# Backward windowed attention with one job per step, and half of the weight gradients computed between its steps

## The chip, the cores and the metric

The kernel runs on one core of a Trainium2 chip. The metric is the device time in microseconds (us) of one execution. All executions of a kernel lie within 1% of its median. Engines are named as in the profile: PE is the matmul engine (TensorE; "PEld" is its weight load), DVE is VectorE, ACT is ScalarE, POOL is GpSimd and SP is SyncE. "ACTq" or "SPq" in front of a DMA is the time in which that engine's instruction stream stands at the *issue* of the DMA; the engine runs no other instruction of its stream meanwhile.

## The reference

Four layers, A B A B, on x of 2048 x 640, each `x = x + layer(layernorm(x))`. A is linear attention, B is softmax attention in a window of 256 positions, both with 32 heads of 20. The kernel returns the output and the gradients of x and of the four weights.

```python
def _B_ref(x, wqkv, wo):                       # A_ref, layernorm: cut
    q, k, v = ...                              # (x @ wqkv), 32 heads of Dh = 20
    scores = einsum("bhqd,bhkd->bhqk", q, k) * Dh ** -0.5
    mask = (i - j >= 0) & (i - j < 256)
    p = softmax(where(mask, scores, -1e9))
    o = einsum("bhqk,bhkd->bhqd", p, v)
    return o... @ wo

def reference(A_x, A_wqkv, A_wo, B_wqkv, B_wo, B_x, grad_out):
    _out, _vjp = jax.vjp(_f, A_x, A_wqkv, A_wo, B_wqkv, B_wo)
    return (_out, *_vjp(grad_out))             # cut
```

## The kernel before

The forward pass comes first (about 900 us). The backward pass then goes through layers 3 (B), 2 (A), 1 (B), 0 (A). For each B layer there is a stage of its own, the attention backward. It walks over 128 units: a unit is four heads (group g of 8) and one block of 128 queries (b of 16), with the at most three key blocks that its window touches. Per unit it recomputes scores and their exponentials `e` (ScalarE), multiplies dP with e into `ds` (VectorE), transposes half of ds by DMA and the other half on PE, and multiplies ds, its transpose and e into dq, dk and dv.

```python
for s in range(n + LAG):                                  # LAG = 5; one step per unit
    if s < n and units[s][1] == 6 and ...: load(units[s][0] + 1)   # slabs of the next group, on ScalarE's queue
    sa = scores(s, 0, "QT", "KT");      pb = scores(s - 2, 1, "dOT", "VT")
    expo(s, 0, sa);                     dscore(s - 2, 1, pb)
    sb = scores(s, 1, "QT", "KT");      pa = scores(s - 1, 0, "dOT", "VT")
    expo(s, 1, sb);                     dscore(s - 1, 0, pa)
    dvk(s - 2, ...)                                       # dk, dv: own accumulator and copy
    if (s - LAG) % 2 == 1: dq([s - LAG - 1, s - LAG])     # dq: own accumulator, in pairs

def dscore(u, half, ps):
    nc.vector.tensor_tensor(out=dv[:, hs], in0=ps..., in1=ev[:, hs], op=ALU.mult)   # ds
    if half == 0:
        self.tr(dsT_of[u]..., ds_of[u]...)                # transposed by DMA
    else:
        for i in range(nb):
            nc.tensor.transpose(tp..., ds_of[u]..., self.ident)   # on PE, right behind its ds
        ...                                               # copied by VectorE or ScalarE in turn
```

dO is loaded once per stage (2.5 MB), and the results of all groups stay on chip in one tile `dqkv`. The next stage (`dh`) transposes that tile and stores it to DRAM for the weight gradients. Those run at the very end, the two layers of a kind in one accumulation:

```python
def weight_grads(self, ls, out_dW, out_dWo):              # called with (3, 1), then (2, 0)
    for m in range(DT):
        ps = pps.tile([P, 512], F32, name="wg")[:, 0:w]
        for i in range(len(ls)):
            for tt in range(TT):
                nc.tensor.matmul(ps, lhsT=lhs[i][:, tt, m * P:(m + 1) * P], rhs=rhs[i][:, tt, :], ...)
        ...                                               # copy to bf16, store
```

The softmax here doesn't subtract the row's maximum and nothing guards it: scores larger than these inputs give would overflow.

## Time and profile before

| | before |
|---|---|
| median of the first 3 runs | 3235.71 us (3222.08 to 3236.21) |
| profiled span | 3230.4 us |
| attention backward, layers 3 and 1 (first score to last product) | 474.1 us each, 3.70 us per unit |
| from the last product to the first matmul of the next stage | 50.1 and 47.3 us |
| weight gradients (first matmul to end) | 421.4 us |

The share of busy time of an engine says little here, since stages have different limits; so here are the windows of the three stages that the change touches. This view gives for each stretch its length, the busy time of PE, PEld, DVE, ACT and POOL with the number of their instructions, then the TensorE clock that was granted (1.00 is full speed), the mean share of time in which DMA engines were busy, and GB/s.

```profile
core 0: us, PE busy (x) PEld busy (x) DVE busy (x) ACT busy (x) POOL busy (x), PEclk, DMA share, GB/s
998.80:1472.90 474.10, 376.98 (x6064) 239.22 (x6063) 258.70 (x320) 280.33 (x496) 147.49 (x240) 0.50 0.58 112
1939.60:2413.70 474.10, 376.62 (x6064) 239.06 (x6064) 258.68 (x320) 280.31 (x495) 147.48 (x240) 0.50 0.58 112
2809.00:3230.40 421.40, 355.53 (x1920) 190.41 (x1920) 21.69 (x36) 12.35 (x24) 0.00 (x0) 0.91 0.45 147
```

No engine is full in the attention stages, and PE runs at half clock throughout, although it is "busy" for 80% of the time. In the weight gradients PE is the limit: 355 us of 421, at nearly full clock.

What PE waits for in layer 3 is in the groups: this view of one line's instructions shows the six transposes of a unit, and what ended PE's idle time before them.

```profile
L745 PEld LDWEIGHTS <-ds x720: 102/147/152, 1004.0 to 1468.1; 128*128 128x128 bf16 x180
L745 PE MATMUL acc<-ident,ds x720: 286/314/314, 1004.0 to 1468.2; 128*128 128x128 bf16 x180
its engine sat idle before it (us, times) until:
  DVE ds L735: 150.6, 195
```

PE and its weight load together sit 150.6 us in front of the transposes, waiting for the ds that VectorE is just writing (the two overlap in part, so it is not a sum of lost time).

The chain that ended last shows the end: matmuls in a row, and between them loads that nothing hides.

```profile
2792.26 16.46 DMA wg_r_38523<-dqkv_118
2808.95 132.40 PE wg L895 x640
...
2950.46 10.38 DMA wg_r_39271<-g_114
...
2961.40 45.14 PE wg L895 x320
```

And between attention and the next stage PE stands idle for 50 us. SP's timeline shows the transposing load of the weight, WT:

```profile
1472.87 40.33 SPq L132 DMA_TRANSPOSE WT_23077<-in_B_wqkv_dram  x1
```

```profile
1472.88 4.91 ACTq L126 DMA_DIRECT2D dqkv_118<-dqkv  x5
```

### The profile page before, as it was taken

To read this page: it belongs to the slowest core of one execution; us is meant where nothing else is said; L and a number is where in the kernel's file an instruction comes from. 1 tells how busy PE (TensorE), PEld (TensorE's weight loads), DVE (VectorE), ACT (ScalarE), POOL (GpSimd) and SP (SyncE) were. 2 spreads that over 40 slices of the span, in tenths; PEclk is the share of its full clock that TensorE was granted. 3 is DMA by queue.
4 is the path that set the end of the run, shared out by engine and by line. 5 is a ranking of instruction groups with operands and counts; after the bars stand their busy time and mean duration, and the time that the engine had idled before them with its cause. 6 is when DMAs were issued, how large, how long until landed. Compare 5 with 4: busy or idle time off the path is not lost. (4 is left out here: it accounts for less than half of the span.)

```text
span 3230.4 us, 64877 instructions
## 1 busy us (share of the span) xinstructions
PE 2348.7 (73%) x26304; PEld 1421.8 (44%) x26304; DVE 1400.7 (43%) x2994; ACT 1160.2 (36%) x2233; POOL 765.5 (24%) x1282
## 2 busy tenths in 40 slices
PE   7599984899744777783846747777774747697797
PEld 5355542454422555552533424554542524344344
DVE  6345543443154555551744645555543735300000
ACT  4167762477603555561101105556550101100000
POOL 0144441255512333331221103333331111000000
PEclk9789986888675555555977875555557968898898
DMA  6788954888597555649879987556469889834624
GB/s 201 204 173 180 195 149 137 177 187 175 138 218 187 116 105 99 120 84 163 185 164 171 239 205 148 96 110 109 93 134 168 172 165 199 259 116 145 205 88 144
DMA packets 992204, 510.50 MB, mean 158 GB/s; under 512 B 818592, under 2 KB 959904, under 8 KB 990624
## 3 DMA queue, kind: packets, MB, share of 16 engines
q1 hardware_dynamic: 738176, 182.81, 36.8%
q10 hardware_dynamic: 242976, 286.83, 29.1%
q0 software_dynamic: 10752, 36.71, 4.7%
q8 instruction: 206, 3.38, 0.4%
q14 instruction: 94, 0.77, 0.1%
HBM read 175.51 MB, written 147.98 MB: 100 GB/s over the span
## 5 line engine op out<-in xcount | busy, mean ns | idle before, releaser
L735 DVE TENSOR_TENSOR ds<-sp,e 128x768 bf16<-128x768 f32 (+2 forms) x512 | 456.4, 906 | 419.5 <-PE sp L702 274.5
L716 ACT ACTIVATE e<-sp 128x768 bf16<-128x768 f32 (+2 forms) x512 | 377.2, 770 | 241.1 <-DMA dOT<-dOT_133 117.4
L343 ACT ACTIVATE e<-s 128x768 bf16<-128x768 f32 (+2 forms) x512 | 374.0, 774 | 140.2 <-PE s L341 109.4
L720 POOL TENSOR_SCALAR_AFFINE_SELECT e<-e 128x512 bf16<-128x512 bf16 x256 | 163.1, 637 | 707.8 <-issue 534.8
L702 PE MATMUL sp<-KT,QT 32*128 32x384 bf16 (+2 forms) x1024 | 247.8, 484 | 95.8 <-DMA VT<-qkvT_132 37.8
L567 PEld LDWEIGHTS <-dqkvT 128*128 128x128 bf16 x1920 | 200.1, 106 | 259.9 <-issue 97.6
L702 PE MATMUL sp<-VT,dOT 32*128 32x384 bf16 (+2 forms) x1024 | 262.0, 471 | 58.2 <-ACT e L716 45.6
L745 PE MATMUL acc<-ident,ds 128*128 128x128 bf16 x1440 | 199.8, 308 | 100.4 <-DVE ds L735 99.6
L346 POOL TENSOR_SCALAR_AFFINE_SELECT e<-e 128x512 bf16<-128x512 bf16 x256 | 163.4, 638 | 398.8 <-ACT e L343 395.4
L569 ACT ACTIVATE dh_junk<-d 128x320 bf16<-128x320 f32 x128 | 56.0, 437 | 505.1 <-PE d L567 492.7
L745 PEld LDWEIGHTS <-ds 128*128 128x128 bf16 x1440 | 132.2, 136 | 210.2 <-DVE ds L735 201.4
L899 DVE CAST wg_r<-wg 128x480 bf16<-128x480 f32 (+1 forms) x36 | 21.7, 603 | 415.1 <-PE wg L895 355.8
L341 PE MATMUL s<-ring 32*128 32x128 bf16 x2880 | 166.0, 234 | 18.5 <-ACT e L343 17.3
L901 ACT CAST wg_r<-wg 128x480 bf16<-128x480 f32 (+1 forms) x24 | 12.4, 515 | 423.3 <-PE wg L895 345.0
L515 PEld LDWEIGHTS <-gT 128*128 128x128 bf16 x640 | 67.6, 112 | 186.0 <-DMA gT<-car 142.7
L349 POOL TENSOR_SCALAR_AFFINE_SELECT e<-e 128x512 bf16<-128x512 bf16 x224 | 143.8, 642 | 0.0
L724 POOL TENSOR_SCALAR_AFFINE_SELECT e<-e 128x512 bf16<-128x512 bf16 x224 | 142.7, 637 | 0.0
L341 PEld LDWEIGHTS <-ring 32*128 32x128 bf16 x2880 | 82.9, 97 | 127.1 <-issue 119.1
L779 ACT CAST dqkv<-acc 128x160 bf16<-128x160 f32 x224 | 70.2, 313 | 190.3 <-PE acc L757 190.3
L215 PEld LDWEIGHTS <-ln_hnT 128*128 128x128 bf16 x960 | 96.1, 106 | 95.1 <-DMA ln_hnT<-ln_hn 37.9
L202 DVE TENSOR_TENSOR car<-d,car 128x320 bf16<-128x320 f32 x128 | 62.2, 486 | 159.2 <-PE d L200 158.8
L702 PEld LDWEIGHTS <-dOT 32*128 32x128 bf16 x1024 | 66.1, 100 | 147.6 <-issue 143.5
(588 smaller groups left out, 4540.6 us busy)
## 6 DMA issues: line engine op xcount, KB each, us to landing
qkvT_128<-ring ACTq DMA_DIRECT2D x16, 768.0 KB, 6.3
qkvT_132<-ring ACTq DMA_DIRECT2D x16, 768.0 KB, 4.4
dqkv_118<-dqkv ACTq DMA_DIRECT2D x16, 480.0 KB, 3.9
dqkv_117<-dqkv_t ACTq DMA_DIRECT2D x16, 480.0 KB, 5.2
dqkv_116<-dqkv ACTq DMA_DIRECT2D x16, 480.0 KB, 4.5
dqkv_115<-dqkv_t ACTq DMA_DIRECT2D x16, 480.0 KB, 4.9
out_dram<-car ACTq DMA_DIRECT2D x32, 160.0 KB, 4.5
out_dram<-wg_r ACTq DMA_DIRECT2D x40, 120.0 KB, 1.7
```

The source lines that it names most:

```text
L215: nc.tensor.matmul(ps, lhsT=hnT[:, k, :], rhs=W[:, k, ci * HD:(ci + 1) * HD], start=(k == 0), stop=(k == self.DT - 1))
L341: nc.tensor.matmul(ps[:, j, i * P:(i + 1) * P], lhsT=ring[r0:r0 + HP, G + g, kt * P:(kt + 1) * P], rhs=ring[r0:r0 + HP, g, qs], start=True ...
L343: nc.scalar.activation(ev[:, 2 * half:2 * half + 2], ps[:, :, 0:nkt * P].rearrange("p h (i q) -> p h i q", q=P), ACT.Exp, scale=self.c_att)
L346: nc.gpsimd.affine_select(out=ev[:, :, nkt - 1, :], in_=ev[:, :, nkt - 1, :], compare_op=ALU.is_ge, fill=0.0, base=0, pattern=[[0, 4], [1, ...
L349: nc.gpsimd.affine_select(out=ev[:, :, 0, :], in_=ev[:, :, 0, :], compare_op=ALU.is_ge, fill=0.0, base=-1, pattern=[[0, 4], [-1, P]], chan ...
L567: nc.tensor.matmul(ps, lhsT=dT[:, k, :], rhs=WT[:, k, cs], start=(k == 0), stop=(k == self.QTT - 1))
L702: nc.tensor.matmul(ps[:, j, 0:nkt * P], lhsT=slabs[g][ta][r0:r0 + HP, b * P:(b + 1) * P], rhs=slabs[g][tb][r0:r0 + HP, k0 * P:(k0 + nkt) * P],
L716: nc.scalar.activation(ev[:, 2 * half:2 * half + 2], ps[:, :, 0:nkt * P].rearrange("p h (i k) -> p h i k", k=P), ACT.Exp, scale=c_att)
L720: nc.gpsimd.affine_select(out=ev[:, :, nkt - 1, :], in_=ev[:, :, nkt - 1, :], compare_op=ALU.is_ge, fill=0.0, base=0, pattern=[[0, 4], [-1 ...
L724: nc.gpsimd.affine_select(out=ev[:, :, 0, :], in_=ev[:, :, 0, :], compare_op=ALU.is_ge, fill=0.0, base=-1, pattern=[[0, 4], [1, P]], chann ...
L735: nc.vector.tensor_tensor(out=dv[:, hs], in0=ps[:, :, 0:nkt * P].rearrange("p h (i k) -> p h i k", k=P), in1=ev[:, hs], op=ALU.mult)
L745: nc.tensor.transpose(tp[:, i * P:(i + 1) * P], ds_of[u][:, (nb + i) * P:(nb + i + 1) * P], self.ident)
```

## The change

The intent: shorten the attention step by taking away its wait for ds, and use the poorly filled PE of layer 1's attention stage for half of the weight gradients (those of layers 3 and 2, whose inputs are complete by then). Scores of one half of the heads are paired with dP of the other half, as they were. The diff, cut to its core:

```diff
+    def permute_w(self):                       # at the start, on SP's queue: B's weight with
+        w = 4 * DH                             # q, k, v of a group side by side (160-byte runs)
+        for t in range(3):
+            self.dma(out[:, t], in_[:, t], self.nc.sync)
@@ dh
-        self.tr(dT, dqkv)
-        self.dma(self.dqkv_d[l][:, tt, :], dqkv)
+        if dqkv is None:
+            self.tr(dT, self.dqkv_d[l][:, tt, :])      # B layers: transposed from DRAM
@@ seg_attention_bwd
-            dO = p1.tile([P, TT, D], BF, name="dO_ld")
-            self.dma(dO, sv["dO"])
@@ load(g): six slabs and now dO's, all on ScalarE's queue
+                r["dO"] = psl.tile([P, TT, 4 * DH], BF, name="dOsl")
+                self.dma(r["dO"], sv["dO"][:, :, 4 * g * DH:4 * (g + 1) * DH])
@@ the step
                 sa = ...; pb = ...; expo(a, 0, sa); dscore(b2, 1, pb)
+                job(s - JL)              # dk, dv and dq of one block, five steps back, one accumulator
+                filling(rate)            # layer 1: 4 weight-gradient matmuls
                 sb = ...; pa = ...; expo(a, 1, sb); dscore(c, 0, pa)
-                dvk(s - 2, ...); dq([...])
+                flip(b2)                 # the PE transposes, out of dscore
+                filling(rate)
@@ job: results leave per group, also on ScalarE's queue
+                if kt == TT - 1:
+                    self.dma(self.dqkv_d[l][:, :, g * 12 * DH:(g + 1) * 12 * DH], outs.pop(g))
@@ run
-                self.seg_attention_bwd(l, dqkv)
+            if l == 3:
+                self.seg_attention_bwd(l, None, 0, 3)          # no fill, 3 score buffers
+            else:
+                    self.seg_attention_bwd(l, it, 4, 2)        # it: wgrad of layers 3, 2
+                    self.drain(it)
-        self.weight_grads((3, 1), ...); self.weight_grads((2, 0), ...)
+            for k in (1, 0):
+                self.drain(self.wgrad(k, pools, True))
@@ wgrad: the first half leaves as fp32 partials in DRAM; the second adds them
+                    if last:
+                        pt = pw.tile([P, 480], F32, name="wg_pt")        # two buffers
+                        self.dma(pt[:, 0:w], part[rows, ...], nc.sync)
+                        nc.vector.tensor_add(o[:, 0:w], ps, pt[:, 0:w])
+                        self.dma(dst, o..., nc.sync)
```

## The prediction

It was made before the changed kernel was built.

> **What bounds the kernel now.** No single engine: the page shows PE 73%, DVE 43%, ACT 36%, DMA unevenly. By stage (windows):
> - The two attention-backward stages run 998 to 1472 and 1940 to 2414 us, 474 us each, 3.70 us per step of 128. PE is busy 79%, ACT 59%, DVE 55%, and the granted clock is exactly 0.50 in every window. The waits there are PE and its weight load waiting for DVE's ds (0.4 and 0.8 us per step: the transposes stand right behind the ds they need) and sp waiting for exp.
> - Weight gradients, 2791 to 3230 us (439 us): 1920 matmuls, clock 0.90. In the chain of waits PE has 355 us (132.4 us per 640 matmuls of 480 columns, 207 ns each); about 80 us are four exposed loads.
>
> **What the change does.**
> 1. Transposes move behind the second score pair, the products become one job five steps back. PE work per step at half clock, estimated from the timeline: two score quads 0.64 us, six transposes 0.64, 36 products of 33 ns 1.2, so about 2.5; ACT about 2.2 and DVE 2.0. With the ds wait gone and three sp buffers I expect 3.05 us per step: about -58 us in layer 3. The 2.5 MB dO load (9.6 to 10.7 us) before the first score goes: -9 us per stage.
> 2. Layer 1's stage gets 8 weight-gradient matmuls per step (about 905 of 960 fit in; the rest hides behind the WT load, 38 to 40 us of SP time). At full clock they cost 1.43 us per step, at half clock 2.9. The skill's page "TensorE: Matmul & The Clock Gate", Part 1, says the throttled state is the default and sustained activity releases it; this trace agrees (0.50 in attention, 1.00 in dense stretches of B-to-A). The fill should release it: scores and transposes halve (0.65 us), products 1.2, fill 1.43, plus about 0.4 for the one wg bank, whose eviction is issued only at the next burst: 3.7 to 3.8 us per step. I expect +10 us less the 9 us of dO.
> 3. The end keeps half the matmuls (177 us of PE), but SP issues both the fp32 partial's load and the output store in order, so a partial's load goes out only after the previous output is ready: about 0.35 + 0.35 + 3 + 0.65 us, 4.3 us per tile against 3.3 of PE; 6 to 6.5 for layer B with its 160-byte output runs. Estimate: 130 + 86 + 2 x 40 + 25 first load and tail = about 290 to 320 us against 439: -150 with some luck in overlap.
> 4. At the start Wp is permuted: 15,360 runs of 160 bytes on SP's queue, ahead of the first LN transposes. "DMA: Bandwidth & Descriptors", Queues, rings and completion order, says descriptors on an engine are consumed in ring order; no view here tests it. 960 per engine at 35 to 60 ns (page: 62 ns per packet on q10): first matmul at 50 us, not 19.8: +30 us.
> 5. dh transposes dqkv from DRAM instead of SBUF; one store moves: about 0. WT's wait stays.
>
> Sum: -58 - 9 + 10 - 9 - 150 + 30 = -186, so about 3045 us.
>
> **Signs.** Layer-3 attention about 410 us, with no ds wait before transposes; layer-1 attention 450 to 540 us with clock above 0.8; end 250 to 320 us with partial loads among its waits; first matmul near 50 us.
>
> **What would make it wrong.** If the fill doesn't release the clock, layer 1 takes 5.5 us per step, +230 us, and the whole is a tie or a loss. ACT could also block on full DMA queues (loads held it 5 to 11 us before). If permutation is cheap and the end PE-bound, 2950.

## The result, and the profile after

The changed kernel has a median of 3073.75 us (3056.17 to 3084.75, 4 runs) against 3235.96 us; the ratio is 0.9489, with a 95% interval of 0.9436 to 0.9542. Ratios in this document are the mean time of one kernel's runs over that of the other's of the same rounds, so they are not quite the ratio of the medians quoted. The prediction's total (about 3045 us) held within 1%. Its terms did not hold as well. The table splits both profiled spans at the same events; "measured" is the difference of the two profiles.

| stretch | before | after | measured | predicted |
|---|---|---|---|---|
| start to first matmul | 19.8 | 35.2 | +15.4 | +30 |
| from there to layer 3's first score | 979.0 | 974.6 | -4.4 | -9 (dO load) |
| layer 3 attention | 474.1 | 457.5 | -16.6 | -58 |
| last product to first dh matmul | 50.1 | 32.0 | -18.1 | 0 |
| layers 3 to 2 to layer 1's first score | 416.7 | 416.1 | -0.6 | -9 (dO load) |
| layer 1 attention, with fill after | 474.1 | 550.2 | +76.1 | +10 |
| last product to first dh matmul | 47.3 | 36.1 | -11.2 | 0 |
| layers 1 to 0 | 347.9 | 354.5 | +6.6 | 0 |
| weight gradients at the end | 421.4 | 198.3 | -223.1 | -150 |
| sum | 3230.4 | 3054.5 | -175.9 | -186 |

(The profiled run of after, 3056 us, is its fastest. The attention stage of layer 1 is the least steady part: runs below that leave its code as it is show 561.0, 569.3 and 571.6 us.)

The windows of the same three stages after the change:

```profile
core 0: us, PE busy (x) PEld busy (x) DVE busy (x) ACT busy (x) POOL busy (x), PEclk, DMA share, GB/s
1009.80:1467.30 457.50, 372.52 (x6064) 237.31 (x6063) 256.31 (x320) 280.37 (x447) 146.88 (x240) 0.50 0.73 126
1915.40:2465.60 550.20, 486.84 (x6944) 279.85 (x6944) 271.83 (x342) 293.99 (x481) 146.93 (x240) 0.88 0.82 171
2856.10:3054.40 198.30, 180.15 (x960) 95.54 (x960) 36.15 (x60) 0.00 (x0) 0.00 (x0) 0.96 0.74 230
```

Layer 3 does the same work at the same clock in hardly less time. Layer 1 has 880 more matmuls in it, and its clock has risen from 0.50 to 0.88. The end is now PE work from one side to the other: 180 of 198 us.

The transposes of layer 3 no longer wait for ds:

```profile
L751 PEld LDWEIGHTS <-ds x720: 102/151/152, 1018.2 to 1463.6; 128*128 128x128 bf16 x180
L751 PE MATMUL tp<-ident,ds x720: 267/314/314, 1018.2 to 1463.7; 128*128 128x128 bf16 x180
its engine sat idle before it (us, times) until:
  issue: 24.6, 75
  DVE ds L742: 4.6, 11
```

150.6 us of waiting became 4.6, and yet the stage lost only 17 us. So the wait must have come back elsewhere. ScalarE's timeline at one change of group shows where (start, duration, engine, then what):

```profile
1192.43 0.61 ACTq L123 DMA_DIRECT2D dqkv<-dqkv_o  x1
...
1196.21 0.34 ACTq L123 DMA_DIRECT2D VT<-qkvT  x1
1196.58 0.75 ACTq L123 DMA_DIRECT2D dOT<-dOT  x1
1197.37 0.62 ACTq L123 DMA_DIRECT2D qsl<-qk  x1
1198.03 8.48 ACTq L123 DMA_DIRECT2D ksl<-qk  x1
1206.56 4.69 ACTq L123 DMA_DIRECT2D dOsl<-dO  x1
1211.37 0.81 ACT L722 ACTIVATE e<-sp 128x768 bf16<-128x768 f32 x1 [14.37 <-issue]
```

Five loads and a store go out on ScalarE's queue within 14 us. The first four issues take under 1 us each, the last two 8.5 and 4.7 us: the stream stands at the issue, and ScalarE computes nothing for 14.37 us before the next exponential. Over the stage, 16 issues of more than 2 us hold ScalarE for 84.3 us; in the kernel before there were 2 of them in this stage, 5.6 us in all. Between such pauses two steps take 5.74 us (2.87 each; one pair of steps runs from 1229.5 to 1235.2 us).

### The profile page after: what moved, and what is told of

Its sections match the earlier page's. It is cut to its first block, busy times and chain, and to the rows that moved or that the text cites. A ratio compares the mean times of both kernels' runs of the same rounds, so it can differ in the third digit from the quotient of the medians.

```text
span 3054.5 us, 65157 instructions
## 1 busy us (share of the span) xinstructions
PE 2301.7 (75%) x26304; PEld 1378.5 (45%) x26304; DVE 1426.9 (47%) x3042; ACT 1162.5 (38%) x2149; POOL 762.9 (25%) x1282
## 4 chain that ended last, share of the span: by engine, by line
PE 51%; DMA 17%; DVE 7%; issue 5%; ACTq 4%; SPq 3%; ACT 3%; POOL 1%; DVEq 0%; POOLq 0%
PE wg L934 10%; PE acc L763 8%; PE sp L708 7%; PE d L575 5%; DMA gT<-car 4%; PE tp L751 4%; ACTq L123 4%; PE d L308 4%; DMA dqkvT<-dqkv_t 3%; SPq L129 3%; PE d L205 3%; PE s L346 3%; PE d L520 2%; PE d L220 2%; PE d L367 1%
## 5 line engine op out<-in xcount | busy, mean ns | idle before, releaser
L722 ACT ACTIVATE e<-sp 128x768 bf16<-128x768 f32 (+2 forms) x512 | 394.1, 773 | 478.0 <-DMA qsl<-qk 175.3
L934 PE MATMUL wg<-wg_r,wg_l 128*128 128x480 bf16 (+1 forms) x1920 | 406.3, 357 | 69.1 <-DMA wg_r<-dqkv 29.5
L575 PE MATMUL d<-WT,dqkvT 128*128 128x320 bf16 x1920 | 317.2, 330 | 132.3 <-DMA dqkvT<-dqkv_t 75.5
L726 POOL TENSOR_SCALAR_AFFINE_SELECT e<-e 128x512 bf16<-128x512 bf16 x256 | 162.4, 634 | 763.5 <-issue 575.9
L934 PEld LDWEIGHTS <-wg_l 128*128 128x128 bf16 x1920 | 180.9, 100 | 214.4 <-issue 72.7
L351 POOL TENSOR_SCALAR_AFFINE_SELECT e<-e 128x512 bf16<-128x512 bf16 x256 | 162.8, 636 | 394.9 <-ACT e L348 391.6
L520 PE MATMUL d<-WoT,gT 128*128 128x320 bf16 x640 | 125.0, 357 | 129.3 <-DMA gT<-car 127.7
L220 PE MATMUL d<-W,ln_hnT 128*128 128x320 bf16 x960 | 163.4, 326 | 66.1 <-DMA ln_hnT<-ln_hn 49.0
L308 PE MATMUL d<-W,ln_hnT 128*128 128x480 bf16 x640 | 189.3, 420 | 0.0
L205 PE MATMUL d<-Wo,oT 128*128 128x320 bf16 x640 | 128.2, 330 | 77.4 <-DMA Wo<-in_A_wo_dram 46.4
L346 PE MATMUL s<-ring 32*128 32x128 bf16 x2880 | 166.5, 234 | 18.3 <-ACT e L348 17.0
L751 PE MATMUL tp<-ident,ds 128*128 128x128 bf16 x1440 | 168.2, 272 | 0.5
L579 DVE CUSTOM_DVE_ANT_0 dh_junk<-d,hn_ld 128x320 bf16<-128x320 f32 x128 | 62.6, 489 | 192.7 <-ACT dh_junk L577 192.4
```

The source lines that it names most:

```text
L220: nc.tensor.matmul(ps, lhsT=hnT[:, k, :], rhs=W[:, k, ci * HD:(ci + 1) * HD], start=(k == 0), stop=(k == self.DT - 1))
L308: nc.tensor.matmul(ps, lhsT=hnT[:, k, :], rhs=W[:, k, ci * 480:(ci + 1) * 480], start=(k == 0), stop=(k == self.DT - 1))
L346: nc.tensor.matmul(ps[:, j, i * P:(i + 1) * P], lhsT=ring[r0:r0 + HP, G + g, kt * P:(kt + 1) * P], rhs=ring[r0:r0 + HP, g, qs], start=True ...
L520: self.nc.tensor.matmul(ps, lhsT=gT[:, k, :], rhs=WoT[:, k, c * self.HD:(c + 1) * self.HD], start=(k == 0), stop=(k == self.DT - 1))
L575: nc.tensor.matmul(ps, lhsT=dT[:, k, :], rhs=WT[:, k, cs], start=(k == 0), stop=(k == self.QTT - 1))
L722: nc.scalar.activation(ev[:, 2 * half:2 * half + 2], ps[:, :, 0:nkt * P].rearrange("p h (i k) -> p h i k", k=P), ACT.Exp, scale=c_att)
```

## The experiments

All runs are compared with the kernel before in rounds of their own. "Ratio" is against the kernel before (after: 0.9489). Stage times come from each run's profile.

| run | what it changes in the changed kernel | median us | ratio (95%) | layer 3 att. | layer 1 att. | end |
|---|---|---|---|---|---|---|
| (after) | | 3073.75 | 0.9489 (0.9436 to 0.9542) | 457.5 | 550.2 | 198.3 |
| e_spread | slab loads spread over steps | 3031.48 | 0.9354 (0.9312 to 0.9395) | 418.6 | 561.7 | 199.4 |
| e_resident | layer 3 loads dO once | 3064.86 | 0.9458 (0.9420 to 0.9497) | 430.0 | 571.6 | 197.3 |
| e_loads_pool | slab loads issued by GpSimd | 3047.95 | 0.9412 (0.9376 to 0.9448) | 416.0 | 566.0 | 199.8 |
| e_loads_sp | slab loads issued by SP | 2957.96 | 0.9139 (0.9097 to 0.9181) | 380.4 | 511.7 | 199.3 |
| e_flip_early | transposes back behind ds | 3090.36 | 0.9573 (0.9500 to 0.9645) | 452.5 | 581.7 | 199.2 |
| f_old_order | e_loads_sp, layer 3 in the old order | 3062.06 | 0.9433 (0.9371 to 0.9494) | 455.3 | 536.6 | 200.0 |
| e_nofill | no fill, two score buffers | 3222.20 | 0.9989 (0.9935 to 1.0043) | 456.0 | 577.9 | 199.6 |
| f_nofill3 | e_loads_sp, no fill, three score buffers | 3065.03 | 0.9451 (0.9386 to 0.9516) | 379.2 | 379.9 | 200.4 |
| f_shared3 | e_loads_sp, third score buffer in layer 1 | 2951.37 | 0.9106 (0.9046 to 0.9166) | 379.1 | 513.9 | 197.1 |
| e_pt1 | one buffer for the fp32 partials | 3185.67 | 0.9874 (0.9814 to 0.9935) | 457.2 | 561.0 | 297.9 |
| e_direct_wt | no permuted copy (wrong) | 3065.63 | 0.9490 (0.9435 to 0.9546) | 456.7 | 569.3 | 199.7 |
| g_best | e_loads_sp, permutation on GpSimd | 2959.85 | 0.9154 (0.9109 to 0.9200) | 379.2 | 519.7 | 197.0 |

All but e_direct_wt compute the right result.

### 1. Where layer 3's gain went: four ways to issue the slab loads

Theory: the bunch of loads on ScalarE's queue stops the exponentials. Rival: the step is held by PE, ScalarE or the DMA traffic itself, and taking the pauses away only moves them.

e_spread issues the same loads on the same queue, one at a time:

```diff
-                if s < n and units[s][1] == 6 and units[s][0] + 1 < G:
-                    load(units[s][0] + 1)
+                if s < n and units[s][0] + 1 < G:
+                    when = {5: "QT", 6: "KT", 7: "VT", 8: "dOT", 9: "q", 11: "k", 13: "dO"}
+                    if units[s][1] in when:
+                        load(units[s][0] + 1, (when[units[s][1]],))
```

> Only the place of the slab loads changes: one load per step or two instead of seven at step 6 of a group. Theory A (the loads, issued in a bunch by ScalarE behind the dqkv store, fill its DMA queue, and ScalarE stands 12 us per change of group at the issue of ksl and dOsl, so the exponentials stop): layer-3 attention (first sp to last product) falls from 458 us to about 390 to 400, no ScalarE issue longer than 2 us in it, and layer 1's stage loses about 30 of its 586 us (first sp to first dh); in all about 2980 us. Rival B (the step is held by PE and ScalarE work or by the DMA traffic itself, and the pauses would only move): layer-3 attention stays within 10 us of 458.

Measured: layer 3's attention fell to 418.6 us; ScalarE's issues of over 2 us went from 16 (84.3 us) to 2 (4.5 us). That is 39 us of the 58 to 68 expected. Layer 1 did not gain (561.7 us), against the expectation.

e_resident takes only dO's slab out of layer 3's bunch, and loads dO once as before:

```diff
-                r["dO"] = psl.tile([P, TT, 4 * DH], BF, name="dOsl")
-                self.dma(r["dO"], sv["dO"][:, :, 4 * g * DH:4 * (g + 1) * DH])
+            if fill is None:                       # once, ahead of load(0)
+                dO = self.pool(st, "at").tile([P, TT, D], BF, name="dO_ld")
+                self.dma(dO, sv["dO"])
```

> Layer 3 loads dO once as before; layer 1 is left. If the new dO slabs (2048 runs of 160 bytes per group) are by themselves the cause of the pauses: layer-3 attention about 400 us and no pause of ScalarE. If the bunch as a whole is (Theory A), only the 3 to 4 us of the dOsl issue go at each of 6 changes of group: about 435 to 440 us, with ksl's issue still at 5 to 8 us, and the first sp some 8 us later because of the 2.5 MB load.

Measured: 430.0 us, with 8 issues of over 2 us left (56.9 us, the longest 9.6). So dO's slab accounts for part of the pauses and the rest of the bunch for more: "the bunch as a whole". The first score came at 1022.3 us instead of 1009.8, and layer 1, whose code is the same, was slower in this run, so the whole gained little.

e_loads_pool and e_loads_sp hand the same loads, at the same place in the program, to another engine:

```diff
-                    self.dma(r[n], sv["qkvT"][:, i * G + g, :])
+                    self.dma(r[n], sv["qkvT"][:, i * G + g, :], nc.sync)     # e_loads_pool: nc.gpsimd
 ... likewise dOT, q, k and dO
```

> The same loads at the same step, issued by GpSimd. Theory A: ScalarE has no pause, layer-3 attention near 395 us, unless GpSimd's own queue holds up the masks (then e waits show, with GpSimd as releaser, and 400 to 430). Rival B: within 10 us of 458.

> The same loads issued by SP, ahead of dsT's transposes. Theory A: ScalarE has no pause; SP is held about 12 us per group instead, which four steps of 2.9 us between a dsT and its use nearly cover: layer-3 attention 400 to 420 us, with waits of PE on dsT. Rival B: within 10 us of 458.

Measured: GpSimd 416.0 us, SP 380.4 us. With SP the ScalarE stream has no issue over 0.6 us in layer 3, and SP takes the pauses without harm (three of its loads stand for over 2 us, 10.5 us in all, and 27 of its transposes, against 10 in after). With GpSimd no issue is long either, but PE waits for the DMA-transposed half of ds (12 times, 33 us of PE waits "DMA dsT<-ds" in its list, longest 5.3 us). The windows of e_loads_sp, layers 3 and 1:

```profile
1013.30:1393.70 380.40, 366.70 (x6064) 235.04 (x6063) 255.54 (x320) 281.29 (x448) 147.24 (x240) 0.50 0.83 152
1852.10:2363.80 511.70, 474.10 (x6943) 273.15 (x6943) 270.22 (x342) 293.78 (x480) 147.28 (x240) 0.93 0.84 185
```

That the pauses reached PE is in its waits for ScalarE's exponentials in layer 3 (us in total, times, longest), after first, then e_loads_sp:

```profile
PE sp L708 <- ACT e L722: 74.3, 9, 11.8
```

```profile
PE sp L708 <- ACT e L722: 2.6, 6, 0.9
```

Layer 3 moves the same work in 77 us less than after, at the same clock, and PE is now busy for 96% of the stage: 2.86 us per step over all 133 steps, what the changed kernel reached only between its pauses. The rival falls, since DMA moves more per second (152 against 126 GB/s) and the step still gets shorter. The expectation for SP (400 to 420 us) was too cautious. e_loads_sp changes the pace of the loads as well as the engine: in its trace the transposes of ds on SP's queue stand between them, so that the seven loads of a group go out over 24 us (1199.9 to 1223.4 us, for one). Why spreading on ScalarE's own queue recovers only half is partly seen in the traces. In e_spread PE waits for exponentials only 4.9 us, so the pauses are gone there too; but the same 6064 matmuls at the same clock keep PE busy for 394.1 us instead of 366.7, because the score matmuls of Q/K and of dO/V run side by side less often (together they take 184.3 us instead of 158.3). So 27 of the 38 us that remain are PE work that came out in a less favourable order; the rest is open.

The Trainium skill, page "DMA: Bandwidth & Descriptors", section "Issuing engines are not separate DMA queues", says that issuing from several engines "will only save the time on the sequencer it takes to initiate the DMA, which is usually small relative to the DMA itself". This case agrees with the first half and is an exception to the second: the time at the issue was 84 us of one stage, on an engine that the stage needs every 1.4 us.

### 2. Is the new order of the step worth anything?

e_flip_early puts only the transposes back behind the ds that they need.

```diff
                     dscore(b2, 1, pb)
+                    flip(b2)
 ...
-                    if 0 <= b2 < n:
-                        flip(b2)
```

> Only the place of the transposes goes back: right behind the ds that they need. If the later place is what shortened the step (2.86 us between loads in layer 3, 3.70 before): PE waits on ds return (0.3 to 0.8 us per step) and layer-3 attention grows by 40 to 70 us. If the wait is filled by other work all the same: within 15 us.

Measured: PE's waits for ds in front of the transposes returned in part (37.5 us against 4.6), but layer 3 took 452.5 us against 457.5. By itself this says that the order is worth nothing. But ScalarE's pauses were still there (16 issues over 2 us, 68.7 us), and could have covered the difference. So the test was made again without them: f_old_order has the loads on SP and gives layer 3 the whole old order, transposes behind ds, dk and dv two steps back in their own accumulator, dq five back in pairs. It takes back the old accumulators with it (two, which transposes and products share, in place of one for each; this part of the edit is left out below).

```diff
                     dscore(b2, 1, pb)
+                    if old: flip(b2)
 ...
+                if old:
+                    dvk(b2, [b - 2, b - 1, b] if b == TT - 1 else [b - 2])    # if b >= 2
+                    if (s - JL) % 2 == 1: dq([s - JL - 1, s - JL])
```

> The loads on SP; layer 3 alone goes back to the order of before (transposes right behind ds, dk and dv two steps back in their own accumulator, dq five back in pairs). If the order is what shortened the step: layer-3 attention 450 to 480 us instead of 380, with PE waiting on ds 0.3 to 0.8 us per step. If the order does little (as the run with early transposes alone hints, 452 against 457 us): 380 to 410.

Measured: 455.3 us against 380.4, with the wait back:

```profile
L751 PE MATMUL acc<-ident,ds x720: 267/314/315, 1019.0 to 1467.3; 128*128 128x128 bf16 x180
its engine sat idle before it (us, times) until:
  DVE ds L742: 112.2, 155
```

So the new order, with its accumulators, is worth 75 us in layer 3 when nothing else holds the step. The whole grew by 104 us, more than that; layer 1, with unchanged code, took 536.6 us against 511.7 (g_best, with the same code there, 519.7), about the spread that this stage shows from run to run. How the 75 us split between the place of the transposes and that of dk and dv was not separated.

### 3. What the fill costs and what it hides

e_nofill was meant as the plain undo: no fill in layer 1, the same 960 matmuls behind it.

```diff
-                    self.seg_attention_bwd(l, it, 4, 2)
+                    self.seg_attention_bwd(l, None, 0, 2)
                     self.drain(it)
```

> No weight gradient inside layer 1's steps; the same 960 matmuls run after its last step, alone. If running them between the steps hides them: this costs about 100 us over the changed kernel (attention about 458 us at clock 0.50 as in layer 3, then about 200 us for 960 matmuls and their loads, 650 to 660 instead of 586 from first sp to first dh). If the fill only adds its own time (rival: nothing hidden): within 20 us of the changed kernel.

Measured: 577.9 us of attention and 176.2 us to the first dh matmul, 754 us in place of 586. But it is no clean undo. The window holds 6443 matmuls where attention has 6064: the framework, which sets the order of each engine's stream itself, had moved some 380 of the later matmuls forward into the stage, at a clock of 0.61.

```profile
1940.10:2518.00 577.90, 524.77 (x6443) 276.70 (x6443) 266.94 (x330) 286.46 (x461) 146.94 (x240) 0.61 0.62 125
```

f_nofill3 opens the weight-gradient buffers only after the stage, so that nothing can move into it, and has the loads on SP and three score buffers.

```diff
+                self.seg_attention_bwd(l, None, 0, 3)
+                with ExitStack() as s2:
+                    pools = self.wg_pools(s2, False)
+                    for k in (3, 2):
+                        self.drain(self.wgrad(k, pools, False))
```

> The loads on SP; layer 1 runs without fill, with three score buffers as layer 3, and the 960 matmuls run after it. The clean undo of the fill: layer-1 attention about 382 us at clock 0.50, then about 205 us of weight gradients, 585 to 595 us from first sp to first dh, against 547 with the fill: in all +40 to +50 us over the run with loads on SP. If the fill hides all 177 us of matmuls (rival): +150 us and more.

Measured: attention 379.9 us and then 284.6 us, 664.5 us in all, against 511.7 + 35.5 = 547.2 us with the fill (e_loads_sp): the fill saves 117 us by stages and 107 us by medians. That lies between theory (+40 to +50) and rival (+150 and more). The stage without fill:

```profile
1843.80:2223.70 379.90, 366.94 (x6064) 235.28 (x6065) 255.56 (x320) 280.86 (x447) 146.97 (x240) 0.50 0.86 151
```

The clock is 0.50 without and 0.93 with the fill. The fill adds 132 us to the stage (0.99 us per step). It takes away 249 us behind it: about 177 us of matmuls at the pace of the end stage (132 + 45 us in the chain of before, for 640 and 320 of them), and the rest loads, the first of each operand (PE waits 9 to 11 us for some of them), and copies for which the one bank makes PE wait (mostly 0.5 to 0.8 us per tile). I had counted about 205 us for that run, and it was 249.

The clock is also seen in single groups. In layer 3 (0.50) six transposes take 0.82 us in a row and a score 0.50 us; with the fill, in this timeline of after at full clock, 0.51 and 0.34:

```profile
2447.44 0.34 PE L708 MATMUL sp<-KT,QT 32*128 32x384 bf16 x2
2447.45 0.34 PE L708 MATMUL sp<-VT,dOT 32*128 32x384 bf16 x2
2447.72 0.51 PE L751 MATMUL tp<-ident,ds 128*128 128x128 bf16 x6
2448.06 0.71 PE L934 MATMUL wg<-wg_r,wg_l 128*128 128x320 bf16 x4
```

f_shared3 gives layer 1 a third score buffer, paid for by letting transposes and products share a bank.

```diff
-                    self.seg_attention_bwd(l, it, 4, 2)
+                    self.seg_attention_bwd(l, it, 4, 3, shared=True)
```

> The loads on SP, and layer 1 gets a third score buffer (paid for by letting transposes and products share one bank). The run without a fill showed two buffers alone cost layer 1 about 120 us (578 against 456 us of attention). If waits for a score buffer still lengthen the filled stage: layer-1 attention falls from 512 us (loads on SP, two buffers) to 460 to 480. If the fill already covers them, or the one shared bank makes new waits between transposes, products and their copies: 500 to 560.

Measured: 513.9 against 511.7 us: no difference. (The premise taken from e_nofill, that two buffers alone cost 120 us, was wrong for the reason just given.) The intervals of f_shared3 and e_loads_sp overlap; they count as equal.

### 4. The end stage: one buffer or two

The prediction had 290 to 320 us for the end (counted from 18 us before the first matmul), because SP would issue the load of a partial only after the store before it. e_pt1 makes that true.

```diff
-                        pt = pw.tile([P, 480], F32, name="wg_pt")
+                        pt = pw.tile([P, 480], F32, name="wg_pt", bufs=1)
```

> One buffer instead of two for the fp32 partials of the last stage, so a partial's load can only go out after the sum before it: the case that my prediction assumed. If my sum was right for that case: the last stage (first wg to end) takes 270 to 300 us instead of 198, in all about +80 us. If the load is quick enough even so (3.7 us to landing, 3.3 us of PE per tile): +10 to +30 us.

Measured: 297.9 us against 198.3. The waits of the two end stages (who waited for whom, us in total, times, longest), e_pt1 first and then after:

```profile
DVE wg_o L941 <- DMA wg_pt<-pq1w: 97.2, 19, 8.8
DVE wg_o L941 <- DMA wg_pt<-pq0w: 82.4, 20, 8.4
PE wg L934 <- DVE wg_o L941: 80.9, 39, 6.0
```

```profile
DVE wg_o L941 <- DMA wg_pt<-pq1w: 34.5, 11, 5.2
DVE wg_o L941 <- DMA wg_pt<-pq0w: 27.7, 8, 8.4
...
PE wg L934 <- DVE wg_o L941: 14.8, 5, 7.7
```

With one buffer PE waits 80.9 us for sums that wait for partials; with two, 14.8. The order on SP is in both traces the one that the prediction had: each partial's load goes out right behind the stores of a tile. What differs is how far ahead it is: with two buffers two loads go out before the first store (from 2843.2 us on, the first store at 2861.9), with one buffer one. So the sum of the prediction was right for a load one tile ahead, and the code's second buffer puts it one tile further.

### 5. The permuted weight: start and WT

e_direct_wt drops the copy and transposes WT from the input. Its gradients are wrong, since dqkv is still in permuted order.

```diff
-            self.tr(t, self.Wp if kind == 1 else self.Wqkv[kind])
+            self.tr(t, self.Wqkv[kind])
 ...
-        self.permute_w()
```

> No permuted copy; WT is transposed from the input itself (two gradients and dx come out wrong on purpose). First matmul back at about 20 us instead of 35 (-15 us). For WT, theory: it took 40 us before because the sixteen 480 KB dqkv stores were issued at the same moment, which are now done inside attention; then it stays at 16 to 20 us here. Rival: the input's place in memory is slow to transpose and the copy is not; then WT takes 38 to 40 us here and the stage gains nothing (+20 us per layer).

Measured: the first matmul comes at 19.4 us instead of 35.2. WT, from the same input as before the change, takes 16.5 us, not 40.3:

```profile
1457.42 16.50 SPq L129 DMA_TRANSPOSE WT<-in_B_wqkv_dram  x1
```

So the source isn't what made WT slow before. What else differs at that moment is the stores of dqkv on ScalarE's queue (480 KB each), which before the change went out together with WT and now leave during attention. That they are the cause is argued from the two traces; no run put only them back. Taken whole, this run is no faster than after (0.9490): the 16 us of the start are lost in layer 1's stage (569.3 us) and other small differences.

g_best puts the copy on GpSimd's queue, beside e_loads_sp's loads.

```diff
-            self.dma(out[:, t], in_[:, t], self.nc.sync)      # permute_w
+            self.dma(out[:, t], in_[:, t], self.nc.gpsimd)
```

> The slab loads on SP, and the permuted copy issued by GpSimd, so that the first LN transposes do not stand behind it in SP's queue. If the queue order is what delayed the first matmul (35 us against 20): it comes back to 20 to 24 us, and the whole falls from 2958 to about 2940 us. If the copy's traffic itself delays the first loads: first matmul stays at 30 us or more and nothing is gained.

Measured: first matmul at 29.7 us, whole 2959.85 us: a third of the delay goes, and the total doesn't change. The traces show what the delay is made of. In after it is not the order of SP's queue: SP has issued the whole copy by 14.4 us, but ScalarE, which issues the loads of x and of A's weight, sends four of them only after a part of the copy has landed (the parts land at 11.8, 16.9 and 24.2 us), so that its first activation of the LN starts at 24.66 us, after 22.57 us of idleness that a DMA of Wp ends. SP's first LN transpose goes out at 25.7 us; without the copy (e_direct_wt) at 9.4. Why the loads wait for the copy was not tested. In g_best they do not, and the transpose goes out at 14.6 us, but it lands 15.1 us later instead of 10.0, while the copy is still moving. Of the versions, e_loads_sp (2957.96 us) and f_shared3 (2951.37 us) beat both kernels, by about 4% over the changed one.

## Why the prediction was right or wrong

The total was right: -162 us by medians against -186. The reasons were right in kind for the two attention stages, where the sizes were off, and in part wrong for the end, the start and dh. That these errors cancel (+41 and +66 us in the two attention stages, -73 at the end, -15 at the start, -29 in front of the two dh, +20 elsewhere) is luck.

1. *"With the ds wait gone and three sp buffers I expect 3.05 us per step: about -58 us in layer 3."* The step came out shorter than that, 2.86 us, and the order with its accumulators is worth 75 us (455.3 against 380.4 us, loads on SP in both). What failed is the balance of the stage: -17 us. Of the 77 us between 457.5 and 380.4, 72 are PE's waits for exponentials (74.3 against 2.6 us), while ScalarE stood at the issue of the slab loads. The prediction named this ("ACT could also block on full DMA queues") and put no number on it. The change itself made it worse: dO's loads and dqkv's stores joined the same queue, and five loads came to stand in a row behind a store. What each of these adds was not separated (without dO's loads, in e_resident, 56.9 of the 84.3 us stay).
2. *"The fill should release it"*: right. Clock 0.88 to 0.93 with the fill, 0.50 without, as the Trainium skill's page "TensorE: Matmul & The Clock Gate", Part 1, has it: throttled by default, released by sustained activity. Activity alone is not enough here, though: in e_loads_sp PE is busy for 96% of layer 3 and the clock stays at 0.50. *"3.7 to 3.8 us per step. I expect +10 us"*: +76 us in the changed kernel, and +38 us once the loads were off ScalarE (511.7 us, 4.00 us for each of 128 units). So a good half of the term's error is again the loads (about 38 us by these two runs, with some 20 us of spread between runs). 28 us remain. In e_loads_sp the fill's matmuls keep PE busy for 211.9 us, 1.66 us per unit and not 1.43, and PE waits 18.3 us for their operands, which the sum left out; against that, the 0.4 us per step for the one bank did not come (1.5 us in all). How these terms add up to the 28 us stays open.
3. *"a partial's load goes out only after the previous output is ready ... -150"*: the step that failed by most. It holds with one buffer (297.9 us from the first matmul on, where e_pt1's expectation put the prediction's sum at 270 to 300); the code has two, and the end took 198.3 us, -223.
4. *"First matmul at 50 us ... +30 us"*: 35.2 us, +15. The packet time was too long: the three DMAs with 15,360 runs had landed 23.4 us after the first was issued, which over 16 engines is 24 ns per run, not 35 to 60. That the copy delays the first matmul is shown (19.4 us without it). The path was another than predicted: the LN transposes waited for the LN, and that for ScalarE's loads, which waited for the copy to land (section 5 of the experiments).
5. *"one store moves: about 0. WT's wait stays"*: wrong. WT went from 40.3 to 16.5 us, and the idle time in front of the next stage from 50.1 to 32.0 us in layer 3 (in layer 1, 38.9 to 20.1 and 47.3 to 36.1). Which of the moved stores and the changed order of issue did it was not tested.

The two smaller signs: the 2.5 MB dO load was worth 4 us to layer 3's first score, not 9. And the fill put 880 matmuls into the stage, where about 905 were expected.

## What to carry to other kernels

Before trusting a shorter step, list what else the engine on it has to do in its stream: here the issue of a load cost 0.3 to 0.8 us at the start of a bunch and 2 to 10 us at the end of a bunch (that its queue was full then is my reading; no view shows it), so such loads are better issued by an engine that the step does not need. When a change takes a wait away and the stage does not get shorter, look for the engine that now stands still, remove that, and only then judge the change: with the pauses in place, early transposes cost nothing, and without them the old order cost 75 us. A stage whose small matmuls leave PE at half clock was here a good place for dense ones (107 us by medians), because they sped up their neighbours as well.

## What the Trainium skill lacked or had wrong

- "DMA: Bandwidth & Descriptors", section "Issuing engines are not separate DMA queues", calls the sequencer's time to initiate a DMA usually small. Behind a bunch of loads it was 8.5 us for a single issue and 84.3 us in one stage, and moving the issues to SP shortened that stage from 457.5 to 380.4 us.
- "TensorE: Matmul & The Clock Gate", Part 1, says that sustained activity releases the throttle, not what counts as activity. Here a PE that by the profile was busy for 80 to 97% of 380 to 474 us, with 32-row scores, transposes and products of 20 columns, stayed at 0.50; eight matmuls of 320 or 480 columns more per step of 3.85 us brought 0.93.
- "DMA: Bandwidth & Descriptors", Specifications, gives 512 bytes as the least transfer for full rate and no time for runs of 160 bytes. From DRAM to DRAM, beside the loads of x, 15,360 such runs landed in 23.4 us, 2.46 MB at about 105 GB/s.
- "DMA: Bandwidth & Descriptors", section "Latency and other measured facts", gives 261 GB/s for a DMA transpose with a non-contiguous middle dimension and 350 to 400 GB/s for the contiguous case, and nothing for one beside other traffic. The same transpose of 2.46 MB took 19.2 us from issue to landing in e_direct_wt and 44.7 us in the kernel before, in which stores of the other queue were issued at the same time: about 128 and 55 GB/s.
